# K transposed in place, with its word pairs dealt to four blocks, in a decode kernel of two attention and MLP layers

## The chip, the cores and the metric

The kernel runs on one core of a Trainium2 chip. A core has several engines that work side by side and wait for each other through semaphores: PE multiplies matrices (in the profile PEld is the loading of its stationary operand, "weights", and PE the multiplication itself), DVE works on vectors and transposes small blocks, ACT computes functions and copies, POOL helps with small things, and SP issues the transfers from the chip's main memory. Data is held in SBUF, 128 partitions of addressable rows, and PE writes its results to PSUM, eight banks of 128 x 512 floats.

The metric is the device time of one execution in microseconds. Smaller is better.

## The reference

Two layers are applied twice with the same weights and the same caches: attention A with cached keys and values, then an MLP-like block B. There are 8 sequences of one new token each, model width 448, 16 query heads over 8 cached heads ("groups" below) of 4096 positions and 256 dimensions.

```python
def _A_ref(x, k_cache, v_cache, wq, wo):
    B, Sq, D = x.shape
    Hq, Dh = 16, 256
    q = (x @ wq).reshape(B, Sq, Hq, Dh).transpose(0, 2, 1, 3)
    k = jnp.repeat(k_cache, 2, axis=1)
    v = jnp.repeat(v_cache, 2, axis=1)
    scores = jnp.einsum("bhqd,bhkd->bhqk", q, k) * (Dh ** -0.5)
    p = _softmax(scores, axis=-1)
    o = jnp.einsum("bhqk,bhkd->bhqd", p, v)
    return o.transpose(0, 2, 1, 3).reshape(B, Sq, Hq * Dh) @ wo

x = A_x
x = x + _A_ref(_layernorm(x), k_cache, v_cache, wq, wo)
x = x + _B_ref(_layernorm(x), w1, w2, w3, w4)
x = x + _A_ref(_layernorm(x), k_cache, v_cache, wq, wo)
x = x + _B_ref(_layernorm(x), w1, w2, w3, w4)
```

With one token per sequence, the part of B that shifts along the sequence yields zeros, and its rest is `gelu(layernorm(x) @ w3) @ w4` with two additions. The caches are nearly all of the data: K and V are 128 MiB each, and both layers read them.

## The kernel before

**Units and parts.** A unit is one pass (1 or 2, the first or the second attention), one sequence and one group: 128 units. The cache rows of a unit are cut into four parts of 512 KB, each a tile of 128 partitions x 2048 bf16 elements (eight positions of 256 dimensions per partition). A part is loaded into one of 31 equal buffers, `slots`.

**K kept for the second pass.** A sequence's pass 1 handles its groups; then its MLP and its second query projection are computed, step by step, beside a few units that belong to other sequences (from `ends` to `fence`); then its pass 2 follows. Six of the eight groups (`KEEP`) keep their transposed K in the slots from pass 1 to pass 2, except for two parts that are parked in PSUM (`park`) and copied back by ACT (line 458). The other two groups (`loose`) load K twice. So units come in two kinds: *fresh* ones load four parts of K and four of V, the others V alone. In order of time there are eight fresh opening units, then in turn a short stretch of four (later three) fresh units with the MLP's steps beside them, and a stretch of twelve units, six of them fresh; the last eight units have two fresh ones.

**Transposing K.** PE contracts over partitions, so the dimensions of K have to lie on partitions. `transposes` (lines 470 to 494) takes a loaded part `raw`, reads it as 4-byte words (pairs of neighbouring bf16 elements), and lets DVE transpose 32 x 32 blocks of words, two instructions of 128 x 512 words each (line 486), into a second slot `kt`. A row of K has 128 words. Before the change, block `e` of a row is its words 32e to 32e+31; both the read and the write run over neighbouring words. Parts that are parked are transposed twice, the second time into PSUM (line 491). The slot `raw` is then free and goes back to the list.

**Slots.** `free` is a list of free slots, in the order in which they were freed. `pump` (line 451) issues the next loads of a fixed list, as long as more than `RESERVE` slots are free: one slot is held back, so that a transposition finds its second slot. The planner's table `by` says how many parts must have been transposed at each quarter of a unit; it spreads a stretch's transpositions evenly over the stretch.

**Scores.** `k_part` (line 565) takes a transposed part in 16 matmuls (line 573). The stationary operand is 128 positions wide: its columns stand two elements apart in `kt` (`x` picks the element of the pair, `e` the block). The moving operand is `Qblk`, which holds the two query heads of the group, zero outside their block of 32 partitions. Then come the softmax (lines 585 to 645, with DVE's reductions in lines 588, 606 and 643) and V's part (line 552), a unit later.

**The queries.** `in_mms` multiplies a token's row by `wq` so that the dimensions of a query come out on partitions; `cols` picks the 128 columns of `wq` that make one matmul. For the queries (`pairs`) it takes every second column out of 256. `expand` (line 148) spreads the result into `Qblk`: four matmuls with 0/1 matrices (`rows32`, line 154) repeat 32 partitions four times, and ACT copies the result into place (line 160).

**Order.** The order on each engine is written out by hand in the main loop: in each quarter of a unit, transpositions, the flush of small steps, scores, softmax, V's part, and one step of the MLP. Each engine works through its own list in order; SP issues the loads in the order in which `pump` was called.

Of the kernel before, what the change touches and what calls it, by code (L numbers as in the profile page):

```python
# [8 lines left out]
FP32 = mybir.dt.float32  # L9
# [5 lines left out]

UNIT = 2048
N_SLOTS = 31
RESERVE = 1
KEEP = 6
PARKED = 2  # L20
RUN = 3
# [5 lines left out]
def kernel(  # L27
# [14 lines left out]
    nc = tc.nc  # L42
# [41 lines left out]
    rows32 = consts.tile([128, 4, 4, 32], BF16, name="rows32")  # L84
# [6 lines left out]
    Qblk = [consts.tile([128, RUN, 4, 2, 4, 2], BF16, name=f"Qblk{i}") for i in range(2)]  # L91
# [4 lines left out]
    scb, dnb, pyb = banks[0:2], banks[2], banks[3]  # L96
    park = [[ps1.tile([128, 512], FP32, name=f"park{i}{q}") for q in range(2)] for i in range(PARKED)]
# [19 lines left out]
    def in_mms(pv, big, tail, rows, n, ms, pairs=False):  # L117

        half = n // 2

        def cols(w, k):
            if pairs:
                return w[:, 256 * (k // 2) + k % 2 : 256 * (k // 2) + 256 : 2]
            return w[:, 128 * k : 128 * k + 128]

        for j, m in enumerate(ms):
            for i in range(2):
                for c in range(3):  # L130
                    nc.tensor.matmul(  # L131
                        pv[:, i, j, :],
                        cols(big[:, c, :], m + i * half),
                        rows[:, c, :],
                        start=(i == 0 and j == 0 and c == 0),
                        stop=True,
                        skip_group_check=True,
                    )
            nc.tensor.matmul(  # L139
                pv[:, :, j, :],  # L140
                cols(tail, m),
                rows[:, 3:5, :],
                start=False,
                stop=True,
                skip_group_check=True,
            )

    def expand(blk, qT, n, bank):

        rp = bank[:, 448 : 448 + 16 * n].rearrange("p (g d e h) -> p g d e h", d=4, e=2, h=2)  # L150
        qs = qT.rearrange("p (g h e) -> p g e h", h=2, e=2)
        for db in range(4):
            sel = rows32[:, db].rearrange("p b i -> p (b i)")
            nc.tensor.matmul(rp[:, :, db], sel, qs, start=True, stop=True)  # L154

        for pb in range(4):
            sl = slice(32 * pb, 32 * pb + 32)
            dst = blk[sl, 0:n, :, :, pb, :].rearrange("p g d e h -> p (g d e) h")
            src = rp[sl].rearrange("p g d e h -> p (g d e) h")
            nc.scalar.copy(dst, src)  # L160
# [188 lines left out]
    parked = {(second[-1], 4 - PARKED + i): i for i in range(PARKED)}  # L349
    early = [(1, b, g) for b in range(1, Bn) for g in loose]  # L350
    after = [(2, b, g) for b in range(Bn - 1) for g in loose]
    units = []
# [15 lines left out]
    def fresh(u, s):  # L368

        return u[0] == 1 or u[2] in loose  # L370
# [4 lines left out]
    t = 0  # L375
    while t < n_units:
        p, b, g = units[t]
        n = 1
# [3 lines left out]
        for j in range(parts_):  # L382
            m = n // parts_ + (j < n % parts_)
# [26 lines left out]
    for t in range(n_units):  # L410
        for s in range(4):
            i = 4 * t + s + LAG
            if t in ends:
                i = 4 * t + (6, 6, 7, 7)[s]
            elif t + 1 == n_units:
                i = 4 * t + (5, 5, 6, 7)[s]
# [4 lines left out]
    k = 0  # L421
    for i in range(4 * n_units + 8):
# [4 lines left out]
        t, q = divmod(i + 2, 4)  # L427
# [3 lines left out]
    free = list(slots)  # L431
    raw_of, v_of, kt_of = {}, {}, {}
# [16 lines left out]
    def pump():  # L449
        while loads and len(free) > RESERVE:  # L450
            kind, t, i = loads.pop()
            _, b, g = units[t]
            x = free.pop(0)
            if kind == "p":
                dst = x[:].rearrange("p (e q c x) -> p q c e x", e=4, q=2, c=4)
                for j in range(2):
                    src = park[parked[g, i]][j][:].bitcast(BF16)
                    nc.scalar.copy(dst[:, j], src.rearrange("p (c e x) -> p c e x", c=4, e=4))  # L458
                kt_of[(1, b, g), i] = x
                continue  # L460
            cache, of = (A_k_cache, raw_of) if kind == "k" else (A_v_cache, v_of)
            nc.sync.dma_start(  # L462
                x[:].rearrange("p (c d) -> p c d", d=Dh),
                cache[b, g].rearrange("(p s c) d -> p s c d", s=4, c=8)[:, i],
            )
            of[t, i] = x
            n_loads[0] += 1
            if n_loads[0] >= 8 and extra:
                nc.sync.dma_start(*extra.pop(0))
# [3 lines left out]
    def transposes(i):  # L473


        while len(parts) - len(todo) < by[i]:
            t, s = todo[-1]
            if 4 * t + s > i and ((t, s) not in raw_of or not free):
                return
            todo.pop()  # L480
            raw = raw_of.pop((t, s))
            kt = kt_of[units[t], s] = free.pop(0)
            src = raw[:].bitcast(FP32).rearrange("p (q c e i) -> p q c e i", q=2, c=4, e=4)
            dst = kt[:].bitcast(FP32).rearrange("p (e q c r) -> p q c e r", e=4, q=2, c=4)
            for q in range(2):
                nc.vector.transpose(dst[:, q], src[:, q])  # L486
            _, b, g = units[t]
            if (g, s) in parked:
                for q in range(2):
                    dst = park[parked[g, s]][q][:].rearrange("p (c e r) -> p c e r", c=4, e=4)  # L490
                    nc.vector.transpose(dst, src[:, q])
            free.append(raw)
            pump()


    pts, scs, mzs, pos = {}, {}, {}, {}
# [9 lines left out]
    def make_blocks(t):  # L506

        if t in runs and t not in ready:
            p, b, g = units[t]
            if p == 1 or b in q_done:  # L510
                x, n = runs[t]
                qT = qT1[:, :, b] if p == 1 else qT2[:, :, b % 3]
                expand(Qblk[x], qT[:, 4 * g : 4 * (g + n)], n, scb[t % 2])
                ready.add(t)

    def head_out(t):
# [25 lines left out]
    def v_part(t, s):  # L542
        if s == 0:
            at = PO + 4 * (t % n_po)
            pos[t] = pyb[:, at : at + 4].rearrange("p (k h) -> p k h", h=2)
            if t == n_po // 2:
                nc.vector.memset(pyb[:, PO : PO + 4 * (n_units - n_po)], 0.0)
        v = v_of.pop((t, s))
        vv = v[:].rearrange("p (c d) -> p c d", d=Dh)
        for c in range(8):  # L550
            for k in range(2):
                nc.tensor.matmul(  # L552
                    pos[t][:, k, :],
                    vv[:, c, 128 * k : 128 * k + 128],
                    pts[t][:, 8 * s + c, :],
                    start=(t == 0 and s == 0 and c == 0 and k == 0),
                    stop=True,
                    skip_group_check=True,
                )
        free.append(v)  # L560
        pump()

    def k_part(t, s):
        u = units[t]
        p, b, g = u
        if s == 0:
            scs[t] = scb[t % 2][:, 0:64].rearrange("p (c b h) -> p c b h", b=4, h=2)
        key = (u if fresh(u, s) else (1, b, g)), s
        ktv = kt_of[key][:].rearrange("p (e c m x) -> p e c m x", e=4, c=2, x=2)
        for c in range(2):  # L570
            for db in range(4):
                for x in range(2):
                    nc.tensor.matmul(  # L573
                        scs[t][:, 2 * s + c, :, :],
                        ktv[:, db, c, :, x],
                        Qblk[run_of[t][0]][:, run_of[t][1], db, x, :, :],
                        start=(db == 0 and x == 0),
                        stop=(db == 3 and x == 1),
                    )
        if p == 2 or g in loose or (g, s) in parked:  # L580
            free.append(kt_of.pop(key))
            pump()
# [117 lines left out]

    pump()
    make_blocks(0)

    last = n_units - 1
    for t in range(n_units + 1):
        cur = t < n_units
        for q in range(4):
            i = 4 * t + q
            if cur:
                if t in fence and q == 0:  # L710
                    while dense:
                        dense_next()
                    flush()
                    make_blocks(t)
                late = q == 0 and t and not beside[t]
                if beside[t]:
                    transposes(i)
                flush()
                if not late and not beside[t]:
                    transposes(i)  # L720
                k_part(t, q)
# [3 lines left out]
            if cur and late:  # L725
                transposes(i)
# [14 lines left out]
            if q > 1:  # L741
                make_blocks(t + 1)
# [36 lines left out]
    for i in (1, 0):  # L779
        f, e = TWICE[i]  # L780
# [24 lines left out]
    for c in range(4):  # L805
        yp = (scb[0] if c % 2 else dnb)[:, 32 * c : 32 * c + Bn]
        for m in range(HC):
# [4 lines left out]
                start=(m == 0),  # L812
                stop=(m == HC - 1),
# [4 lines left out]
    for c in range(4):  # L818
        sel = ident if c < 3 else rows32[:, 2:4, 0, :]
# [37 lines left out]
```

## Time and profile before

| | |
|---|---|
| median of 3 runs | 1136.29 us (1134.88 to 1136.89) |
| the profiled execution | 1134.93 us, its span 1133.2 us |
| busy PE / PEld / DVE / ACT / POOL | 689.6 / 624.5 / 556.7 / 293.1 / 104.2 us |
| read from main memory | 446.77 MB, 394 GB/s over the span |
| transpositions of K into slots (line 486) | 640, 415.9 us of DVE, 688 ns each |
| transpositions into the park (line 491) | 32, 20.4 us |
| score matmuls (line 573) | 8192, with 8192 weight loads of 104 ns each, overlapping |

The profile is of one execution. Its groups are instructions of one line with one shape: number, busy time, mean duration, and the idle time of the engine just ahead of them with what ended it. The durations of one engine's instructions can overlap: 16 weight loads of 104 ns each are issued in 0.43 us. A stage's row gives the busy time of each engine in a stretch of the span.

### The profile page before, as it was taken

The page shows a single profiled execution, that of the slowest core. Times are in us where ns is not written, and L with a number is a line of the kernel's source. Part 1 is how long each engine was busy: PE and PEld are TensorE (multiplying, and loading weights), DVE is VectorE, ACT ScalarE, POOL GpSimd, SP SyncE. Part 2 cuts the span into 40 slices and gives each one's busy share as a digit, 9 for nine tenths or more (in the row PEclk, how much of TensorE's full clock was granted, in tenths as well). Part 3 has the DMA queues.
Part 4 walks back from the last instruction along what each step waited for, and adds up shares of the span by engine and source line. Part 5 has one row for each costly group of instructions (what it writes and reads, how often), then busy time and mean ns, then how long its engine had stood idle before and what let it go on. Part 6 is the DMA issues. An engine that isn't in the chain of part 4 may idle for free.

```text
span 1133.2 us, 46689 instructions
## 1 busy us (share of the span) xinstructions
PE 689.6 (61%) x20665; PEld 624.5 (55%) x20665; DVE 556.7 (49%) x1305; ACT 293.1 (26%) x1280; POOL 104.2 (9%) x156
## 2 busy tenths in 40 slices
PE   3155665657656576565656666565765666565665
PEld 3144655556555565565655565565655565565665
DVE  5265645446454554545545464545544454546332
ACT  1012123222322223221232214222232214221241
POOL 0000010001000010000000010000100000000011
DMA  9999999999999999999999999999999999999993
GB/s 362 383 418 417 407 399 416 417 405 387 417 417 416 398 392 415 416 417 374 402 417 416 417 375 387 417 417 415 358 416 416 416 384 409 417 416 406 355 417 132
DMA packets 127194, 449.80 MB, mean 397 GB/s; under 512 B 13568, under 2 KB 19600, under 8 KB 126608
## 3 DMA queue, kind: packets, MB, share of 16 engines
q1 hardware_dynamic: 126992, 446.83, 98.9%
q8 instruction: 161, 2.64, 0.8%
q14 instruction: 41, 0.34, 0.1%
HBM read 446.77 MB, written 0.01 MB: 394 GB/s over the span
## 4 chain that ended last, share of the span: by engine, by line
DMA 71%; PE 13%; DVE 5%; issue 5%; ACT 3%; SPq 2%; POOL 0%; POOLq 0%; DVEq 0%; ACTq 0%
DMA slot<-in_A_v_cache_dram 42%; DMA slot<-in_A_k_cache_dram 28%; PE bank L552 3%; DVE slot L486 3%; PE bank L573 3%; PE bank L131 2%; SPq L462 2%; ACT pt L636 2%; PE bank L231 1%; PE bank L632 1%; ACT pe L609 1%; DVE small L606 1%; PE bank L596 0%; PE bank L622 0%; PE bank L139 0%
## 5 line engine op out<-in xcount | busy, mean ns | idle before, releaser
L552 PE MATMUL bank<-pt,slot 128*128 128x2 bf16 x8192 | 302.0, 166 | 361.3 <-DMA slot<-in_A_v_cache_dram 327.3
L552 PEld LDWEIGHTS <-slot 128*128 128x128 bf16 x8192 | 265.6, 105 | 414.7 <-DMA slot<-in_A_v_cache_dram 380.4
L486 DVE STREAM_TRANSPOSE slot<-slot 128x512 f32<-128x512 f32 x640 | 415.9, 688 | 146.7 <-DMA slot<-in_A_k_cache_dram 131.6
L573 PE MATMUL bank<-Qblk,slot 128*128 128x8 bf16 x8192 | 294.9, 168 | 24.2 <-issue 15.4
L573 PEld LDWEIGHTS <-slot 128*128 128x128 bf16 x8192 | 263.7, 104 | 28.7 <-issue 22.5
L644 POOL TENSOR_TENSOR small<-small 128x2 f32<-128x2 f32 x128 | 89.3, 698 | 970.7 <-DVE small L643 970.7
L609 ACT ACTIVATE pe<-bank,small 128x32 bf16<-128x32 f32 x256 | 61.1, 296 | 449.9 <-DVE small L606 449.9
L636 ACT CAST pt<-bank 32x64 bf16<-32x64 f32 x512 | 103.8, 203 | 142.8 <-PE bank L632 138.4
L606 DVE TENSOR_REDUCE small<-bank 128x2 f32<-128x256 f32 x128 | 54.0, 422 | 154.0 <-PE bank L596 154.0
L643 DVE TENSOR_REDUCE small<-bank 128x2 f32<-128x64 f32 x128 | 28.4, 221 | 160.9 <-ACT pt L636 119.6
L588 DVE TENSOR_REDUCE small<-bank 128x2 bf16<-128x64 f32 x128 | 27.2, 213 | 88.1 <-PE bank L573 88.0
L160 ACT CAST Qblk<-bank 32x48 bf16<-32x48 f32 (+2 forms) x200 | 37.4, 187 | 101.1 <-PE bank L154 87.3
L632 PE MATMUL bank<-pe,rows 128*128 128x64 bf16 x512 | 51.0, 241 | 0.0
L596 PE MATMUL bank<-rows,small 128*128 128x128 bf16 x256 | 48.0, 291 | 1.9 <-DVE small L588 1.9
L522 ACT ACTIVATE OT<-bank,small 128x2 bf16<-128x2 f32 x128 | 26.9, 261 | 70.1 <-PE bank L552 68.9
L175 PEld LDWEIGHTS <-wo_sb 128*128 128x128 bf16 x1152 | 35.4, 104 | 6.8 <-issue 6.8
L632 PEld LDWEIGHTS <-rows 128*128 128x128 bf16 x512 | 33.7, 124 | 8.6 <-issue 7.5
L175 PE MATMUL bank<-OT,wo_sb 128*128 128x1 bf16 x1024 | 33.1, 165 | 5.0 <-ACT OT L522 5.0
L131 PEld LDWEIGHTS <-wq_sb 128*128 128x128 bf16 x864 | 29.9, 106 | 8.5 <-DMA wq_sb<-in_A_wq_dram 4.5
L622 PE MATMUL bank<-pe,small 128*128 128x64 bf16 x128 | 27.3, 213 | 7.2 <-ACT pe L609 4.4
L458 ACT COPY slot<-park 128x1024 bf16<-128x1024 bf16 x32 | 30.8, 1015 | 3.1 <-PE bank L552 2.9
L522 ACT ACTIVATE qT<-bank,small 128x2 bf16<-128x2 f32 x128 | 27.0, 265 | 7.8 <-PE bank L552 4.2
(108 smaller groups left out, 321.3 us busy)
## 6 DMA issues: line engine op xcount, KB each, us to landing
slot<-in_A_v_cache_dram SPq DMA_DIRECT2D x512, 512.0 KB, 9.9
slot<-in_A_k_cache_dram SPq DMA_DIRECT2D x320, 512.0 KB, 9.9
wo_sb<-in_A_wo_dram SPq DMA_DIRECT2D x4, 896.0 KB, 9.3
wq_sb<-in_A_wq_dram SPq DMA_DIRECT2D x3, 1024.0 KB, 6.9
w_sb<-in_B_w_dram SPq DMA_DIRECT2D x1, 1568.0 KB
w_sb<-in_B_w_dram SPq DMA_DIRECT2D x3, 448.0 KB, 10.3
wq_tl<-in_A_wq_dram SPq DMA_DIRECT2D x2, 256.0 KB, 10.1
w_tl<-in_B_w_dram SPq DMA_DIRECT2D x2, 112.0 KB, 9.3
```

The source lines that it names most:

```text
L131: nc.tensor.matmul(pv[:, i, j, :], cols(big[:, c, :], m + i * half), rows[:, c, :], start=(i == 0 and j == 0 and c == 0), stop=True, skip_ ...
L175: nc.tensor.matmul(y[:, c, :], chunk(wo_sb[:, k, :], c), o[:, k, :], start=False, stop=True, skip_group_check=True,)
L486: nc.vector.transpose(dst[:, q], src[:, q])
L522: nc.scalar.mul(o, pos[t][:, :, h], rzs[t % 2][:, h : h + 1])
L552: nc.tensor.matmul(pos[t][:, k, :], vv[:, c, 128 * k : 128 * k + 128], pts[t][:, 8 * s + c, :], start=(t == 0 and s == 0 and c == 0 and k ...
L573: nc.tensor.matmul(scs[t][:, 2 * s + c, :, :], ktv[:, db, c, :, x], Qblk[run_of[t][0]][:, run_of[t][1], db, x, :, :], start=(db == 0 and x ...
L596: nc.tensor.matmul(mzs[t][:, 128 * h : 128 * h + 128], pm[:, h : h + 1].to_broadcast([128, 128]), ident, start=True, stop=True,)
L606: nc.vector.tensor_reduce(nm, mx, AX.X, ALU.max, negate=True)
L609: nc.scalar.activation(pe[:].rearrange("p c b h -> p h (c b)")[:, h], scs[t].rearrange("p c b h -> p h (c b)")[:, h], ACT.Exp, bias=nm[:, ...
L632: nc.tensor.matmul(pp[:, c], sel, pe[:], start=True, stop=True)
L636: nc.scalar.copy(pts[t][sl].rearrange("p (k c) h -> p k c h", c=4), pp[sl, :, :, pb, :].rearrange("p c k h -> p k c h"),)
L644: nc.gpsimd.tensor_tensor(out=rzs[t % 2], in0=zs, in1=mone, op=ALU.pow)
```

## The change

The blocks of a row are chosen differently. Words are dealt to the four blocks in turn: block `e` of a row now consists of words e, e+4, e+8 and so on. Read and write of the transposition use the same pattern, so the block is written over itself in the slot in which it was loaded; no second slot is taken, the slot is not freed after the transposition but only after its scores, and `RESERVE` is 0. A part that is parked is first transposed into the park and then in place. In the scores the stationary operand's columns stand eight elements apart instead of two. To match, `cols` takes every eighth column out of 1024 of `wq`, so that a matmul's result holds four heads with 32 partitions each, and `expand` takes, for each of the four heads, the rows that hold it: a matmul for each block of 32 partitions, over the groups of one parity. The numbers of loads, their order, and the places of all transpositions in DVE's list stay the same.

```diff
-RESERVE = 1
+RESERVE = 0
...
         def cols(w, k):
             if pairs:
-                return w[:, 256 * (k // 2) + k % 2 : 256 * (k // 2) + 256 : 2]
+                return w[:, 1024 * (k // 8) + k % 8 : 1024 * (k // 8) + 1024 : 8]
             return w[:, 128 * k : 128 * k + 128]
...
-    def expand(blk, qT, n, bank):
+    def expand(blk, qT, g0, n, bank):
 
         rp = bank[:, 448 : 448 + 16 * n].rearrange("p (g d e h) -> p g d e h", d=4, e=2, h=2)
-        qs = qT.rearrange("p (g h e) -> p g e h", h=2, e=2)
-        for db in range(4):
-            sel = rows32[:, db].rearrange("p b i -> p (b i)")
-            nc.tensor.matmul(rp[:, :, db], sel, qs, start=True, stop=True)
+        rq = bank[:, 448 : 448 + 16 * n].rearrange("p (g x h) -> p g x h", x=8, h=2)
+        for k in range(4):
+            gs = [g for g in range(g0, g0 + n) if g % 2 == k // 2]
+            if gs:
+                sel = rows32[:, k].rearrange("p b i -> p (b i)")
+                qs = qT[:, 8 * (gs[0] // 2) : 8 * (gs[-1] // 2) + 8]
+                nc.tensor.matmul(
+                    rq[:, gs[0] - g0 : gs[-1] - g0 + 1 : 2, :, k % 2],
+                    sel,
+                    qs.rearrange("p (g x) -> p g x", x=8),
+                    start=True,
+                    stop=True,
+                )
...
             if kind == "p":
-                dst = x[:].rearrange("p (e q c x) -> p q c e x", e=4, q=2, c=4)
                 for j in range(2):
                     src = park[parked[g, i]][j][:].bitcast(BF16)
-                    nc.scalar.copy(dst[:, j], src.rearrange("p (c e x) -> p c e x", c=4, e=4))
+                    nc.scalar.copy(x[:, 1024 * j : 1024 * j + 1024], src)
...
             t, s = todo[-1]
-            if 4 * t + s > i and ((t, s) not in raw_of or not free):
+            if 4 * t + s > i and (t, s) not in raw_of:
                 return
             todo.pop()
             raw = raw_of.pop((t, s))
-            kt = kt_of[units[t], s] = free.pop(0)
-            src = raw[:].bitcast(FP32).rearrange("p (q c e i) -> p q c e i", q=2, c=4, e=4)
-            dst = kt[:].bitcast(FP32).rearrange("p (e q c r) -> p q c e r", e=4, q=2, c=4)
-            for q in range(2):
-                nc.vector.transpose(dst[:, q], src[:, q])
+            kt_of[units[t], s] = raw
+            src = raw[:].bitcast(FP32).rearrange("p (q c i e) -> p q c e i", q=2, c=4, e=4)
             _, b, g = units[t]
             if (g, s) in parked:
                 for q in range(2):
-                    dst = park[parked[g, s]][q][:].rearrange("p (c e r) -> p c e r", c=4, e=4)
+                    dst = park[parked[g, s]][q][:].rearrange("p (c i e) -> p c e i", c=4, e=4)
                     nc.vector.transpose(dst, src[:, q])
-            free.append(raw)
-            pump()
+            for q in range(2):
+                nc.vector.transpose(src[:, q], src[:, q])
...
-                expand(Qblk[x], qT[:, 4 * g : 4 * (g + n)], n, scb[t % 2])
+                expand(Qblk[x], qT, g, n, scb[t % 2])
...
-        ktv = kt_of[key][:].rearrange("p (e c m x) -> p e c m x", e=4, c=2, x=2)
+        ktv = kt_of[key][:].rearrange("p (c m e x) -> p e c m x", e=4, c=2, x=2)
```

## The prediction

> **What bounds the kernel now.** I read the page's sections on queues and on the chain first, then the costly groups, then the table by stage.
>
> ```profile
> span 1133.2 us, 46689 instructions
> ...
> PE 689.6 (61%) x20665; PEld 624.5 (55%) x20665; DVE 556.7 (49%) x1305; ACT 293.1 (26%) x1280; POOL 104.2 (9%) x156
> ...
> q1 hardware_dynamic: 126992, 446.83, 98.9%
> ...
> DMA 71%; PE 13%; DVE 5%; issue 5%; ACT 3%; SPq 2%; POOL 0%; POOLq 0%; DVEq 0%; ACTq 0%
> ...
> L486 DVE STREAM_TRANSPOSE slot<-slot 128x512 f32<-128x512 f32 x640 | 415.9, 688 | 146.7 <-DMA slot<-in_A_k_cache_dram 131.6
> L573 PE MATMUL bank<-Qblk,slot 128*128 128x8 bf16 x8192 | 294.9, 168 | 24.2 <-issue 15.4
> L573 PEld LDWEIGHTS <-slot 128*128 128x128 bf16 x8192 | 263.7, 104 | 28.7 <-issue 22.5
> ```
>
> The loads bound the kernel: the transfer engines are busy for 98.9% of the span, and the chain that ended last is 71% DMA. DVE works half of the time, and three quarters of that is L486, the transposition of K. At 417 GB/s, the best rate of a slice, 446.83 MB need 1072 us, so 61 us of the span are not at the full rate. Where they are, the table by stage shows. I cut the span at the ends of units (the 128 reductions of L588), at the points where the planner cuts its rows. The first row is the eight opening units; then follow, in the order of time, a stretch of four units that load K, a stretch of twelve of which six load K, a stretch of three, and the last eight units. All instructions come first, L486 alone last:
>
> ```profile
> 0.00:107.30 107.30, 41.78 (x1177) 35.86 (x1177) 53.05 (x125) 17.88 (x76) 6.55 (x16) 1.00 1.01 394
> 107.30:148.80 41.50, 27.82 (x827) 25.66 (x827) 24.67 (x67) 8.63 (x42) 4.04 (x6) 1.00 1.02 405
> 284.10:377.30 93.20, 56.72 (x1717) 50.53 (x1715) 43.85 (x91) 27.53 (x118) 8.37 (x12) 1.00 1.03 417
> 647.90:683.30 35.40, 22.93 (x689) 21.36 (x690) 18.88 (x56) 6.31 (x30) 3.34 (x5) 1.00 0.99 383
> 1059.90:1113.30 53.40, 36.71 (x1177) 35.34 (x1175) 16.68 (x40) 19.58 (x80) 5.59 (x8) 1.00 1.00 395
> ...
> 107.30:148.80 41.50, 19.61 (x31) 1.00 1.02 405
> 284.10:377.30 93.20, 32.41 (x50) 1.00 1.03 417
> ```
>
> Columns: stretch, length, busy PE, PEld, DVE, ACT, POOL, granted clock, DMA share, GB/s. In the twelve-unit stretches the loads run at 417 and nothing else matters. In the short ones (four of four units, mean 42.2 us; four of three, mean 34.4 us) they drop to 380 to 405: there the MLP's steps alternate between PE and DVE, and slots come free late. DVE is nearest to its limit there, with 24.67 of 41.50 us.
>
> **What the new access costs.** K's blocks are now read and written with one 4-byte word in every 16 bytes, and so are the weights of L573 and of the q projection (one 2-byte element in every 16 bytes). Before, both were contiguous, or had a step of two elements. No transposition or weight load of the trace has a step of 16 bytes. The nearest rows are these:
>
> ```profile
> L686 DVE COPY X<-bank 128x32 f32<-128x32 f32 x1 | 0.3, 266 | 0.0
> L692 DVE CAST slot<-bank 128x24 bf16<-128x24 f32 x1 | 0.2, 181 | 1.3 <-PE bank L690 1.3
> L824 DVE CAST slot<-bank 8x256 bf16<-8x256 f32 x1 | 0.4, 412 | 0.3 <-PE bank L820 0.3
> L772 DVE CAST slot<-slot 128x32 bf16<-128x32 f32 x1 | 0.2, 228 | 0.0
> L797 DVE TENSOR_TENSOR slot<-slot,slot 128x32 f32<-128x32 f32 x1 | 0.2, 192 | 0.7 <-POOL slot L784 0.7
> ...
> L154 PE MATMUL bank<-qT,rows x4: 182/183/183, 17.1 to 17.2; 128*128 128x12 bf16 x4
> L154 PE MATMUL bank<-qT,rows x4: 175/175/176, 85.2 to 85.3; 128*128 128x8 bf16 x4
> L154 PE MATMUL bank<-qT,rows x4: 172/172/173, 171.2 to 171.3; 128*128 128x12 bf16 x4
> ```
>
> These are rows by line and form, and one line's instructions in three windows (the third reads qT2, 6 bytes apart). L692 and L824 write contiguously: 231 ns for 232 more elements, 1.0 ns each, so 32 elements would take 189 ns. L686 writes 32 floats 16 bytes apart in 266 ns: 77 ns more, 3.4 ns an element. L772 writes elements 16 bytes apart in 228 ns against 192 ns for the same number in L797: 2.1 ns an element. PE reads qT1 with a step of 16 bytes in L154: four more columns cost 8 ns, 2.0 ns each. So 2.0 to 3.4 ns an element in place of 1.0. I take 2.4, nearer to the two that agree. Both streams of a transposition are strided now; I count them as running side by side, and what they cost if they add up is a rival.
>
> [...]
>
> **Part by part.**
>
> *Transposition, L486 and the parked copies.* 640 and 32 instructions, as many as before and in the same places, except that a parked block is now copied ahead of its own transposition. One costs 19.61/31 = 0.633 us of DVE now, and 0.633 + 512 x 1.4 ns = 1.35 us then (bounds: 0.633 if steps are free, 0.633 + 512 x 2.4 ns = 1.86 us). DVE's other work in a stage is its row less L486. To it come the waits for PE that DVE keeps in each unit's softmax: the groups of L606, L643 and L588 idle 154.0, 160.9 and 88.1 us over 128 units, 3.1 us a unit. Much of this is only slack; I keep 1.2 us a unit, L606's part.
> - Four-unit stretch: 5.1 + 31 x 1.35 + 4.8 = 51.8 us, against 42.2: +9.6, four times: 38.
> - Three-unit stretch: 4.5 + 23 x 1.35 + 3.6 = 39.2 us, against 34.4: +4.8, four times: 19.
> - Twelve-unit stretch (50 transpositions and 4 copies to the park): 9.0 + 54 x 1.35 + 14.4 = 96.3 us, against 92.3: +4, seven times: 28.
> - First stage: work on K begins at 14.7 us; 14.7 + 7.8 + 70 x 1.35 + 2 = 119 us, against 107.3: +11.7.
> - Last stage: 16.7 + 16 x 0.72 = 28 of 53 us: nothing.
> Together 97 us. What is late then: reductions queue behind transpositions of 2.7 us a part, PE waits for transposed K, and slots come free late, so SP's loads wait. DVE takes DMA's place as the bound of the short stretches.
>
> *Weight loads of L573 and of the q projection.* 8192 and 1008. They issue 0.43 us per 16 now, 27 ns each, with a step of two elements, just as V's contiguous ones in L552. [...] I take 53 ns, doubled, near to what PE's own strided read shows in L154. A twelve-unit stretch then has 56.7 + 768 x 0.027 = 77 us of PE work, a four-unit one 27.8 + 352 x 0.027 = 37 us, below DVE's 96 and 52: hidden, as long as DVE is the slower one. Not hidden: 112 loads ahead of the first scores, 3 us, and in the last stage 50.4 us of PE work in 53.4 us, where I put 3 us. Together 6.
>
> *One slot.* A block needs no second slot, and none is held back: all 31 slots hold loads, one more than now, 1.26 us of loading (512 KB at 417 GB/s). SP's queue has the same loads in the same order. What goes is its wait for L486 to release a slot (67.5 us in 71 waits); the slot is released by PE's scores instead, and SP waits for those. Where DVE bounds, loading ahead is worth nothing: 0 us. Bounds: 0, and the 29 us that the rate's dips cost between the first 60 and the last 35 us (windows of 20 us, each one's shortfall from 417 GB/s).
>
> *The rest.* Building the query blocks takes eight matmuls fewer (0.2 us), some with 16 columns in place of 12, and writes PSUM with a step of two words; 44 waits of ACT stand behind it, so at most 1 us either way. ACT's copies out of the park (32 x 1.015 us) keep their number of elements: 0, inside ACT's 74% idle time. The transposition's wait for a free slot goes (10.7 us of idle DVE on PE), which pays only where DVE bounds, and is within the kept 1.2 us.
>
> The sum: 97 + 6 = 103 us on the profiled execution's 1134.9 us (span 1133.2 and 1.7 around it; 1.4 below the median of the runs): 1238, stated as 1240.
>
> **Rivals.**
>
> *Steps cost little, the slot decides (faster).* If an element takes at most about 1.9 ns, a transposition is under 1.1 us, a four-unit stretch 5.1 + 34 + 4.8 = 44 us at most, and with steps free nothing is lost; each of the eight dips then gets a block of 1.26 us more to live on, perhaps twice. 1134.9 - 8 x 1.26 = 1125 us; 1105 if all 29 us come back. This turns to slower once an element costs 2 ns. Against it stand L686, L772 and L154. [...]
>
> *Mild.* 2.0 to 2.2 ns: a transposition of 1.15 to 1.25 us, hidden in the twelve-unit stretches, and 6 us or less in each short one: 1139 us, with the slot's gain, to 1180.
>
> *Heavy.* From 2.8 ns up: L686's 3.4 ns, or reads and writes that add up: 1.86 us. The four stages' sums grow by 25, 16, 31 and 47 us: 100 + 66 + 220 + 47 = 433, 1568 us; at 3 ns (1.66 us) about 1435.
>
> [...]
>
> **How the numbers follow.** The forecast (2.2 to 2.7 ns) has 0.45, on its own 1180 to 1340 us, by the same four sums; mild 0.12; heavy 0.15; weight loads 0.08; the faster case 0.20, of which 0.03 falls within 0.2% of no change (about 2.3 us, what a measurement here can tell). Faster 0.17, same 0.03, slower 0.80. The range leaves out the lowest of the faster case (0.08) and most of the two heavy ones (0.12): 1122 to 1430.
>
> **What would show it.** L486's mean: 688 ns now, about 1.4 us if right, under 1.1 if the faster rival holds, near 1.9 if the heavy one does. [...] DVE's busy share: 49% now, near 85%. The rate in the short stretches falls to about 310 GB/s, and there the chain goes through DVE L486 instead of DMA. I am wrong if transpositions with a step keep their time, or if DVE's part of the softmax costs much more than 1.2 us a unit once it is full.

## The result, and the profile after

The changed kernel takes 1166.81 us (1165.79 to 1168.16, 4 runs), the kernel before 1135.59 us beside it: 1.0277 times as long, 95% interval 1.0257 to 1.0297, so 31 us slower. Slower was forecast, but by 104 us.

From the page of the changed kernel: busy times, the load queue, the chain that ended last, and the groups that answer to those shown of before (lines have moved: L486 is now L498, L573 is L578).

```profile
span 1164.0 us, 46597 instructions
...
PE 968.8 (83%) x20657; PEld 929.3 (80%) x20657; DVE 813.9 (70%) x1305; ACT 294.4 (25%) x1280; POOL 104.3 (9%) x156
...
q1 hardware_dynamic: 126992, 446.83, 96.8%
...
DMA 58%; PE 21%; DVE 15%; issue 2%; SPq 2%; ACT 1%; POOL 0%; POOLq 0%; DVEq 0%; ACTq 0%
...
L498 DVE STREAM_TRANSPOSE slot<-slot 128x512 f32<-128x512 f32 x640 | 678.5, 1119 | 50.4 <-DMA slot<-in_A_k_cache_dram 49.6
L578 PE MATMUL bank<-Qblk,slot 128*128 128x8 bf16 x8192 | 574.9, 202 | 25.6 <-DVE slot L498 18.6
L578 PEld LDWEIGHTS <-slot 128*128 128x128 bf16 x8192 | 543.5, 167 | 30.3 <-DVE slot L498 23.7
L131 PEld LDWEIGHTS <-wq_sb 128*128 128x128 bf16 x864 | 62.7, 169 | 4.3 <-DMA wq_sb<-in_A_wq_dram 4.3
```

A transposition takes 1119 ns where it took 688. A score weight load takes 167 ns where it took 104, and 16 of them are issued in 0.97 us instead of 0.43. PE and DVE together got 536 us more to do; the kernel lost 31. The chain says where: DMA's share falls from 71% to 58%, DVE's rises from 5% to 15% and PE's from 13% to 21%.

The same stretches as in the prediction, cut at the ends of units of the changed kernel (columns as there): the eight opening units, a four-unit, a twelve-unit and a three-unit stretch, and the last eight units.

```profile
0.00:109.90 109.90, 64.86 (x1217) 60.03 (x1217) 79.17 (x125) 17.86 (x76) 6.57 (x16) 1.00 1.01 397
245.20:291.70 46.50, 38.64 (x805) 37.12 (x803) 36.18 (x67) 8.89 (x42) 4.04 (x6) 1.00 0.98 382
291.70:383.10 91.40, 79.97 (x1745) 76.62 (x1742) 64.98 (x91) 27.25 (x116) 8.37 (x12) 1.00 1.02 410
657.30:697.10 39.80, 32.28 (x665) 30.82 (x663) 27.18 (x56) 6.33 (x30) 3.34 (x5) 1.00 0.93 362
1088.00:1144.40 56.40, 52.92 (x1179) 52.09 (x1177) 22.88 (x41) 19.52 (x80) 5.58 (x8) 1.00 0.94 366
```

| profiled execution | first | eight short | seven long | last | rest |
|---|---|---|---|---|---|
| before | 107.3 | 306.4 | 646.2 | 53.4 | 19.9 |
| changed | 109.9 | 343.8 | 634.3 | 56.4 | 19.6 |

The short stretches, where the MLP runs beside fresh units, lose 37.4 us. The long ones *gain* 11.9. Neither PE (39 of 46.5 us) nor DVE (36) fills a short stretch, which is the first thing to explain.

### The profile page after: what moved, and what is told of

It is laid out like the page before. It is cut to its first block, busy times and chain, and to the rows that moved or that the text cites. A ratio compares the mean times of both kernels' runs of the same rounds, so it can differ in the third digit from the quotient of the medians.

```text
span 1164.0 us, 46597 instructions
## 1 busy us (share of the span) xinstructions
PE 968.8 (83%) x20657; PEld 929.3 (80%) x20657; DVE 813.9 (70%) x1305; ACT 294.4 (25%) x1280; POOL 104.3 (9%) x156
## 4 chain that ended last, share of the span: by engine, by line
DMA 58%; PE 21%; DVE 15%; issue 2%; SPq 2%; ACT 1%; POOL 0%; POOLq 0%; DVEq 0%; ACTq 0%
DMA slot<-in_A_v_cache_dram 38%; DMA slot<-in_A_k_cache_dram 18%; DVE slot L498 11%; PE bank L578 10%; PE bank L557 4%; PE bank L131 4%; SPq L470 1%; DMA w_sb<-in_B_w_dram 1%; DVE small L611 1%; DVE park L496 1%; PE bank L139 1%; PE bank L601 1%; DMA wq_sb<-in_A_wq_dram 1%; PE bank L184 1%; PE bank L240 0%
## 5 line engine op out<-in xcount | busy, mean ns | idle before, releaser
L498 DVE STREAM_TRANSPOSE slot<-slot 128x512 f32<-128x512 f32 x640 | 678.5, 1119 | 50.4 <-DMA slot<-in_A_k_cache_dram 49.6
L578 PE MATMUL bank<-Qblk,slot 128*128 128x8 bf16 x8192 | 574.9, 202 | 25.6 <-DVE slot L498 18.6
L578 PEld LDWEIGHTS <-slot 128*128 128x128 bf16 x8192 | 543.5, 167 | 30.3 <-DVE slot L498 23.7
L557 PEld LDWEIGHTS <-slot 128*128 128x128 bf16 x8192 | 279.3, 106 | 134.3 <-DMA slot<-in_A_v_cache_dram 128.4
L131 PEld LDWEIGHTS <-wq_sb 128*128 128x128 bf16 x864 | 62.7, 169 | 4.3 <-DMA wq_sb<-in_A_wq_dram 4.3
L131 PE MATMUL bank<-small,wq_sb 128*128 128x1 bf16 x768 | 55.4, 198 | 0.0
L496 DVE STREAM_TRANSPOSE park<-slot 128x512 f32<-128x512 f32 x32 | 33.9, 1108 | 0.0
```

The costliest lines, as they stand in the source:

```text
L131: nc.tensor.matmul(pv[:, i, j, :], cols(big[:, c, :], m + i * half), rows[:, c, :], start=(i == 0 and j == 0 and c == 0), stop=True, skip_ ...
L498: nc.vector.transpose(src[:, q], src[:, q])
L557: nc.tensor.matmul(pos[t][:, k, :], vv[:, c, 128 * k : 128 * k + 128], pts[t][:, 8 * s + c, :], start=(t == 0 and s == 0 and c == 0 and k ...
L578: nc.tensor.matmul(scs[t][:, 2 * s + c, :, :], ktv[:, db, c, :, x], Qblk[run_of[t][0]][:, run_of[t][1], db, x, :, :], start=(db == 0 and x ...
```

## The experiments

Three accesses have become strided: the transpositions (T below), the score weights (K) and the wq columns (W). The first two theories blame one engine each: in the expectations, theory T means the transpositions on DVE, and theory W all weight loads on PE, those of K and of wq. Four kernels undo the three accesses one at a time, and all at once. The kernel before, run beside each of the kernels below, took 1133.4 to 1133.8 us, beside the result 1135.6; so a difference of 1 or 2 us between kernels measured apart is not to be read.

**Score weights two elements apart again**

```diff
-        ktv = kt_of[key][:].rearrange("p (c m e x) -> p e c m x", e=4, c=2, x=2)
+        ktv = kt_of[key][:].rearrange("p (e c m x) -> p e c m x", e=4, c=2, x=2)
```

> The changed kernel, with the weights of the score matmuls read two elements apart again. The blocks stay dealt by fours, so the scores add products of dimensions that do not belong together; the amount of work is the same. Theory W (the weight loads cost the time: 66 ns in place of 32 each, in PE's list): L578's weight loads fall back to about 104 ns in mean and 0.43 us per 16, the short stretches fall from 46.5 and 39.8 us to about 42 and 35, the first and last stage lose their 3 us each, and the time is 1128 to 1142 us. Theory T (the transpositions cost the time: DVE's 1.12 us each, ahead of the MLP's steps in DVE's list): short stretches stay at 45 to 46.5 and 38 to 40 us, time 1155 to 1167 us.

Measured: 1153.6 us, 1.0173 times before (1.0150 to 1.0197). K's weight loads are back at 105 ns; 13 us came back.

**Transpositions over neighbouring words, still in place**

```diff
-            src = raw[:].bitcast(FP32).rearrange("p (q c i e) -> p q c e i", q=2, c=4, e=4)
+            src = raw[:].bitcast(FP32).rearrange("p (q c e i) -> p q c e i", q=2, c=4, e=4)
...
-                    dst = park[parked[g, s]][q][:].rearrange("p (c i e) -> p c e i", c=4, e=4)
+                    dst = park[parked[g, s]][q][:].rearrange("p (c e r) -> p c e r", c=4, e=4)
```

> The changed kernel, with the transpositions over neighbouring words (blocks of 32 words side by side, still in place). The weights are still read eight elements apart, so the scores add products of dimensions that do not belong together; the amount of work is the same. Theory T: L498 falls to about 690 ns, the short stretches to about 42 and 35 us, time 1128 to 1142 us. Theory W: L498 falls all the same, but the time stays at 1155 to 1167 us. If both prices matter in about equal parts, this run and the one with cheap score weights each lie near 1150.

Measured: 1147.76 us, 1.0116 (1.0087 to 1.0144); 19 us came back. The chain on its page shows that DVE is out of it and PE, at 29%, is not:

```profile
DMA 65%; PE 29%; SPq 2%; ACT 2%; issue 1%; DVE 1%; POOL 0%; POOLq 0%; ACTq 0%; DVEq 0%
...
L498 DVE STREAM_TRANSPOSE slot<-slot 128x512 f32<-128x512 f32 x640 | 413.4, 685 | 102.2 <-DMA slot<-in_A_k_cache_dram 102.1
```

**wq columns two apart**

```diff
-                return w[:, 1024 * (k // 8) + k % 8 : 1024 * (k // 8) + 1024 : 8]
+                return w[:, 256 * (k // 2) + k % 2 : 256 * (k // 2) + 256 : 2]
```

> The changed kernel, with the columns of wq taken two apart, as before. The queries' dimensions then stand in another order than K's; the amount of work is the same. The 112 weight loads of each second query projection fall from about 60 ns to 27 ns each, 3.7 us in each short stretch and once at the start. Theory W, with the projection on the stretch's chain: 8 x 3 to 4 us and 3 us at the start, 1132 to 1143 us. Theory T: at most 10 us, 1157 to 1167 us.

Measured: 1147.21 us, 1.0114 (1.0087 to 1.0140); 20 us came back, as much as from the transpositions, and from 1008 weight loads against K's 8192.

**All three undone: the slot alone**

The three edits above together.

> The changed kernel without any of its strided reads: transpositions in place over neighbouring words, score weights and wq columns two elements apart. The scores add products of dimensions that do not belong together; the amount of work is the same. What is left of the change is the slot. If the slot is worth what the faster rival said (a block of 1.26 us in each of eight dips), 1120 to 1128 us; if a slot is worth nothing, 1133 to 1138 us.

Measured: 1131.45 us, 0.9974 (0.9961 to 0.9987), 2 to 3 us faster than before. That lies between the two cases of the expectation: the slot helps, by less than a third of what the faster rival gave it.

So neither theory stood: each access alone gave back 13 to 20 us, 52 in sum, where undoing all gave back 35. Either prices hide behind each other, or something absorbs the first of them. The next three kernels keep one strided access each.

**Only the transpositions strided**

```diff
-                return w[:, 1024 * (k // 8) + k % 8 : 1024 * (k // 8) + 1024 : 8]
+                return w[:, 256 * (k // 2) + k % 2 : 256 * (k // 2) + 256 : 2]
...
-        ktv = kt_of[key][:].rearrange("p (c m e x) -> p e c m x", e=4, c=2, x=2)
+        ktv = kt_of[key][:].rearrange("p (e c m x) -> p e c m x", e=4, c=2, x=2)
```

> One slot and in place, with only the transpositions strided: score weights and wq columns are read two elements apart, so the scores add products of dimensions that do not belong together; the amount of work is the same. Removed from the whole change one at a time, the three strided accesses gave back 13 (score weights), 19 (transpositions) and 20 us (wq), 52 together, where removing all gave back 35. Theory C (one chain: the MLP's steps of a short stretch pass through DVE and PE in turn, so that every price on it adds up): each access alone costs its share of 35, here 12 to 19 us over the slot alone, 1143 to 1150 us. Theory S (slack: each alone is covered by the loads, and only two together exceed them): 0 to 6 us, 1131 to 1138 us.

Measured: 1136.52 us, 1.0024 (1.0006 to 1.0042): 5 us over the slot alone.

**Only the score weights strided** (the changed kernel with the edits of T and W undone, as above)

> One slot and in place, with only the score weights strided (eight elements apart); transpositions run over neighbouring words and wq columns are taken two apart, so the scores add products of dimensions that do not belong together; the amount of work is the same. Theory C: 8 to 13 us over the slot alone, 1139 to 1145 us. Theory S: 0 to 4 us, 1131 to 1136 us.

Measured: 1132.83 us, 0.9994 (0.9976 to 1.0012): 1 us over the slot alone.

**Only the wq columns strided** (the edits of T and K undone)

> One slot and in place, with only the wq columns strided (eight apart); transpositions over neighbouring words and score weights two elements apart, so the queries' dimensions stand in another order than K's; the amount of work is the same. Theory C: 13 to 20 us over the slot alone, 1144 to 1152 us. Theory S: 0 to 6 us, 1131 to 1138 us.

Measured: 1134.83 us, 1.0015 (1.0000 to 1.0029): 3 us over the slot alone.

Theory S (slack, in the expectations above) holds in the total: alone, 5, 1 and 3 us by the medians, 2 to 6 by the ratios; together 35. The stretches of the profiled executions, one for each kernel, in us, show that theory C (one chain) holds as well, in the short ones:

| strided | eight short | over the slot alone | seven long | time |
|---|---|---|---|---|
| none (the slot alone) | 301.9 | | 643.0 | 1131.45 |
| K | 312.1 | 10.2 | 632.5 | 1132.83 |
| T | 314.4 | 12.5 | 634.6 | 1136.52 |
| W | 315.7 | 13.8 | 634.3 | 1134.83 |
| T, K | 324.2 | 22.3 | 634.8 | 1147.21 |
| T, W | 333.8 | 31.9 | 635.7 | 1153.60 |
| K, W | 334.6 | 32.7 | 628.5 | 1147.76 |
| T, K, W | 343.8 | 41.9 | 634.3 | 1166.81 |

In the short stretches the prices add up, or come to more: T and K 22.7, measured 22.3; T and W 26.3, measured 31.9; K and W 24.0, measured 32.7; all three 36.5, measured 41.9. The long stretches give some 7 to 15 us back, once, and the second and third access get nothing more from them. The first 10 us or so that the short stretches lose are thus nearly free: while they are late the loads go on as long as there are slots, and the long stretches start further ahead. The rates show it. By rate times length, the eight short stretches move 229 blocks of 512 KB with the slot alone and 236 to 241 with one strided access; the seven long ones, which use 504 blocks, move 505 with the slot alone, 495 to 499 with one strided access and 491 in the changed kernel. Why they give back no more is not shown. It is not that they stand at the full rate of the loads: 504 blocks of 1.257 us are 633.5 us, near the 634 of most rows, but K and W together need only 628.5, and the long stretches of the changed kernel run at 399 to 412 GB/s, not 417. In one of them, 429.6 to 520.0, the dip comes at its start: from 429.6 to 440.0 the rate is 372 GB/s and PE is busy for 10.39 of 10.40 us, and after that the rate is 415 to 418.

**Why the prices add up although neither engine is full.** The chain through the short stretch from 520.0 to 566.5 us of the changed kernel (start, length, what), its DVE part and then some of its PE part:

```profile
535.74 2.07 DVE slot L498 x2
537.81 0.10 DVE small L226
...
538.53 2.13 DVE slot L498 x2
...
540.86 1.34 DVE slot L498 x2
...
546.21 2.07 DVE slot L498 x2
...
553.43 0.59 PE bank L240 x2
554.01 0.36 PE bank L131 x6
554.38 0.06 PE bank L139
...
556.54 0.96 PE bank L578 x16
557.50 0.23 PE bank L601 x2
557.73 0.40 PE bank L557 x16
558.13 0.37 PE bank L131 x6
```

And the engines' busy times in the two parts of it:

```profile
535.00:553.40 18.40, 15.20 (x338) 14.54 (x335) 17.92 (x45) 3.95 (x19) 2.09 (x3) 1.00 0.97 373
553.40:566.50 13.10, 13.07 (x243) 13.07 (x244) 7.15 (x10) 2.82 (x13) 1.26 (x2) 1.00 0.96 355
```

Up to 535 us the stretch waits for loads (the chain stands on a block of V until 531.7). The rest has two parts with a full engine each. As long as the MLP's steps stand in DVE's list among the transpositions, DVE is busy for 17.92 of 18.40 us. Then comes the second query projection, and PE is busy for 13.07 of 13.10 us, with wq's weight loads and K's in turn. Over the whole stretch PE is busy for 38.55 and DVE for 36.06 of 46.5 us, as if each had about a fifth of its time to spare.

That this is so in all eight short stretches, and which access lengthens which part, the other profiled executions show. Each short stretch is cut here at the first matmul of the second query projection (L131), and the eight are summed, in us:

| strided | up to the projection | from there on |
|---|---|---|
| none (the slot alone) | 240.3 | 61.5 |
| K | 245.9 | 66.3 |
| T | 259.1 | 55.1 |
| W | 240.1 | 75.8 |
| T, K | 261.5 | 62.8 |
| T, W | 257.6 | 76.1 |
| K, W | 247.1 | 87.6 |
| T, K, W | 256.3 | 87.6 |

T lengthens only the first part, and W only the second. K costs 6 us in the first, and in the second 5 us without W but 12 beside it. With K and W strided, PE is busy for the whole of the second part in all eight stretches, and T changes nothing in it. In the 18 us ahead of the cut DVE is busy for 98% in the four-unit and 90% in the three-unit stretches of the changed kernel, and for 66 to 77% with K and W alone. Only a part of each price counts, though. T makes the 31 or 23 transpositions of a stretch 13 or 10 us longer (0.43 us each), of which the first parts show 1.2 to 2.4 us a stretch in the mean. That fits the wait for loads up to 535 us: as long as it lasts, a longer transposition is covered.

**The small steps ahead of the transpositions**

```diff
-                if beside[t]:
-                    transposes(i)
                 flush()
-                if not late and not beside[t]:
+                if not late:
                     transposes(i)
```

> The whole change, with the MLP's small steps put ahead of the transpositions in DVE's list in the short stretches too (as they are elsewhere). If the steps are late in the short stretches because they stand behind two transpositions of 1.1 us each, this shortens the short stretches by 1 to 3 us each, 1145 to 1160 us. If DVE then waits for PE ahead of the transpositions instead, and the scores wait for the blocks, the short stretches stay or grow, 1166 to 1185 us.

Measured: 1167.37 us, 1.0306 (1.0268 to 1.0343), the same as the changed kernel. Where the steps stand in DVE's list does not matter for the time. An engine that is full whatever the order would explain that; this run does not prove it.

**The changed kernel with one slot less**

```diff
-N_SLOTS = 31
+N_SLOTS = 30
```

> The whole change with 30 slots, so that the loads have as many slots as before the change. If the slot is worth the same here as without the strided accesses (2 to 3 us there), 1168 to 1171 us; if it is worth a block's load in each of the eight short stretches, which are late now, 1175 to 1180 us; if nothing, 1166 to 1168 us.

Measured: 1176.85 us, 1.0380 (1.0356 to 1.0404): 10 us more than with 31. The profiled stretches: short 346.1 us, long 642.9, against 343.8 and 634.3. So the slot is worth 10 us here: the time of the expectation's second case, but most of it in the long stretches and not in the short ones. With as many slots for loads as before, the strided accesses cost 43 us; the slot the change gains pays for 10 of them.

**The kernel before with one slot less** (the same edit)

> The kernel before with 30 slots, one less. A slot was worth 2 us without strided accesses (in place against two slots) and 10 us in the whole change. If a slot's worth rises with how late the short stretches are, it is worth 2 to 4 us here, 1135 to 1139 us; if the number of slots itself matters and 30 are just too few, 1142 to 1147 us.

Measured: 1142.19 us, 1.0073 (1.0046 to 1.0100), 8 us more. Without strided accesses each slot is worth less than the one before: 8 us for the 31st of the old kernel, 2 to 3 for the one that in-place work adds to it. So the number of slots counts, as the second case of the expectation has it. It is not all that counts: the step from 30 to 31 slots for loads is worth 2 to 3 us without the strided accesses and 10 with them, which points to the lateness of the short stretches as well.

**What the strided accesses cost by themselves.** Two kernels show it line by line. The first is the kernel before, with one side of each transposition strided:

```diff
-            dst = kt[:].bitcast(FP32).rearrange("p (e q c r) -> p q c e r", e=4, q=2, c=4)
-            for q in range(2):
-                nc.vector.transpose(dst[:, q], src[:, q])
+            far = raw[:].bitcast(FP32).rearrange("p (q c i e) -> p q c e i", q=2, c=4, e=4)
+            fat = kt[:].bitcast(FP32).rearrange("p (q c i e) -> p q c e i", q=2, c=4, e=4)
+            near = kt[:].bitcast(FP32).rearrange("p (q c e r) -> p q c e r", q=2, c=4, e=4)
+            nc.vector.transpose(near[:, 0], far[:, 0])
+            nc.vector.transpose(fat[:, 1], src[:, 1])
```

> The kernel before with two slots, where the first transposition of a part reads one word in four and writes neighbouring words, and the second reads neighbouring words and writes one word in four. The blocks of the two halves are laid out differently, so the scores add products of dimensions that do not belong together; the amount of work is the same. In the whole change, where both are strided, one took 1119 ns against 688. If reads and writes run side by side and cost the same, both lines show about 1.1 us; if only one side costs, one line stays at 690 ns and the other shows about 1.1 us; if they add, each shows about 0.9 us.

Its groups (L487 reads strided and writes neighbours, L488 the other way round):

```profile
L487 DVE STREAM_TRANSPOSE slot<-slot 128x512 f32<-128x512 f32 x320 | 347.9, 1087 | 83.3 <-DMA slot<-in_A_k_cache_dram 74.6 <-PE bank L554 2.6 <-issue 2.3
L488 DVE STREAM_TRANSPOSE slot<-slot 128x512 f32<-128x512 f32 x320 | 340.8, 1065 | 0.0
```

Either side alone costs nearly as much as both (1119 ns): the two prices do not add up, as if reads and writes ran side by side. The kernel takes 1147.85 us, one run, 14 us more than the kernel before. In place, with one slot more for loads, strided transpositions alone came to 1136.52 us; that too speaks for a slot that is worth more where the short stretches are late.

The second is the slot alone, with four steps for the score weights:

```diff
...
+                    kk = kt_of[key][:]
+                    to = scs[t][:, 2 * s + c, :, :]
+                    qb = Qblk[run_of[t][0]][:, run_of[t][1], db, x, :, :]
+                    if db == 0:
+                        nc.tensor.matmul(to, kk[:, 256 * c + x : 256 * c + 256 : 2], qb, start=(x == 0), stop=False)
+                    elif db == 1:
+                        nc.tensor.matmul(to, kk[:, 512 * c + x : 512 * c + 512 : 4], qb, start=False, stop=False)
+                    elif db == 2:
+                        nc.tensor.matmul(to, kk[:, 1024 * c + x : 1024 * c + 1024 : 8], qb, start=False, stop=False)
+                    else:
+                        nc.tensor.matmul(to, kk[:, 8 * c + x : 2048 : 16], qb, start=False, stop=(x == 1))
```

> One slot, transpositions over neighbouring words, and the score weights read with four steps on four lines: 2, 4, 8 and 16 elements (4, 8, 16 and 32 bytes). The scores add products that do not belong together; the amount of work is the same. Step 2 shows 104 ns and step 8 about 167 ns in mean. If what counts is that two neighbouring columns share a 16-byte line, step 4 stays at 104 ns and step 16 is as dear as step 8; if the price grows with the step, step 4 lies between 104 and 167 ns and step 16 above 167.

From its timeline (start, length of the group, line); L582, L584, L586 and L588 have steps of 2, 4, 8 and 16 elements, two loads each:

```profile
302.50 0.13 PEld L582 LDWEIGHTS <-slot 128*128 128x128 bf16 x2
302.55 0.15 PEld L584 LDWEIGHTS <-slot 128*128 128x128 bf16 x2
302.61 0.21 PEld L586 LDWEIGHTS <-slot 128*128 128x128 bf16 x2
302.72 0.22 PEld L588 LDWEIGHTS <-slot 128*128 128x128 bf16 x2
302.84 0.15 PEld L582 LDWEIGHTS <-slot 128*128 128x128 bf16 x2
302.92 0.15 PEld L584 LDWEIGHTS <-slot 128*128 128x128 bf16 x2
```

From start to start, two loads take 0.05, 0.06, 0.11 and 0.12 us. In mean over the run's 2048 loads of each line, one lasts 111, 116, 155 and 162 ns. A part of a dear load's time seems to fall to the load behind it: the two loads of step 2 take 0.05 us to the next start when they follow V's (302.50 to 302.55), and 0.08 when they follow those of step 16 (302.84 to 302.92). So a step of 4 elements (8 bytes) is free or nearly so, 0.06 against 0.05 us; 8 and 16 elements (16 and 32 bytes) cost about the same, 0.11 and 0.12 us, twice as much and a little more. The times fall as in the expectation's first case; that lines of 16 bytes are the reason, the run does not show. The kernel takes 1133.41 us, one run.

## Why the prediction was wrong

- **The sign, and that 16-byte steps cost time on DVE and PE:** right. The faster rival's turning point, 2 ns an element, was wrong: at 1.84 ns the kernel is 31 us slower. The measured time lies in the stated range, but outside the forecast's own 1180 to 1340 us. It is among the mild rival's times, but not by its reasons: at 1.84 ns the price is the faster rival's (at most about 1.9), and the time is not.
- **"So 2.0 to 3.4 ns an element in place of 1.0. I take 2.4":** too high, and the bounds too. (1119 - 688)/512 = 0.84 ns more make 1.84 ns. Copies of 32 elements were a poor measure; the nearest row, 2.0, was PE's, another engine's, which is luck. That the prices of the two streams do not add up was right (1087 and 1065 ns for one side, 1119 for both).
- **The sum by stages, 97 us:** this is the step that failed. It set the work of one engine, DVE, against the whole length of a stretch. With the right price, 0.633 + 0.43 = 1.06 us, the same sums give 42.8 us for a four-unit stretch (then 42.2), 32.5 for a three-unit one (34.4), 81 for a long one (92.3) and 98.7 for the first (107.3): nearly nothing. The profiled stretches are 45.0 to 46.5, 39.8, 90.6 in mean and 109.9. So the price was too high, and behind it a term was missing: DVE fills only the first part of a short stretch and PE the second, and what lengthens either part lengthens the stretch, whichever engine has the larger sum. By the runs, T costs 5 us alone and 19 beside K and W (1166.81 against 1147.76), where 97 were forecast; K and W together cost 30 us beside T (1166.81 against 1136.52), where 6 were.
- **"Hidden, as long as DVE is the slower one" (weight loads, 6 us):** wrong. K and W together cost 32.7 us in the short stretches, without T 16 us in the time. The price, taken as 53 ns, is 61 (0.97 us per 16). The 0.08 for weight loads as the bound rests on no price that a run shows: steps of 16 and 32 bytes cost at most these 61 ns a load, and with them PE is busy for 80 of 91 us in a long stretch. The 112 loads of wq in a stretch were put beside DVE; they are on the chain after DVE's part has ended. They got 112 x 34 ns = 3.8 us longer, and the second part of a stretch shows 1.8 to 3.1 us of it. In the last stage 3 us were forecast and 3.0 came, in part by chance: with the slot alone, nothing strided, it is already 55.3 us against 53.4.
- **Long stretches, +4 us each:** they got 1.7 us shorter each. At 1.12 us a transposition DVE fills 65 of 91 us there, and the chain through one of them (429.6 to 520.0) is 90% loads.
- **"Where DVE bounds, loading ahead is worth nothing: 0 us":** wrong, since it does not bound the long stretches. The slot is worth 10 us in the changed kernel, as much as the faster rival gave it but for another reason, and 2 to 3 us without the strided accesses, which is that rival's case.
- **What was to show it:** L498's mean lies between the mild and the faster case, DVE is busy for 70% (85 forecast), the short stretches run at 360 to 382 GB/s (310 forecast). That the chain would go through DVE's transpositions there was right for the first part of a stretch.

## What to carry to other kernels

When steps of two engines alternate, cut the stretch finer until one engine is full in each piece; 83% of PE and 78% of DVE over a whole stretch can be two pieces at 100 and 97%, and then both prices count. This kernel, bound by its loads, took a small delay for next to nothing, while free slots let the loads run ahead, so single costs of 1 to 5 us made 35 together. Before an in-place layout is chosen for the sake of a buffer, ask for what a buffer is worth (here 2 to 3 us) and for the step that it forces on every reader (here 16 bytes: 1119 ns against 688 for DVE's transposition, 1.6 times, and 0.97 us against 0.43 for 16 of PE's weight loads, 2.3 times).

## What the runs showed of the hardware

- A weight load of 128 columns takes 27 ns from start to start at a step of 4 bytes (0.43 us per 16, kernel before), about 30 at 8 bytes (0.06 us for two, the four steps on four lines), and 55 to 61 ns at 16 and 32 bytes (0.97 us per 16 in the changed kernel; 0.11 and 0.12 us for two in the other).
- A transposition of 128 x 512 words takes 688 ns over neighbouring words and 1065 to 1119 ns with one word in four on either side or both. The second side adds 3 to 5%.
- One more slot of 512 KB for loads was worth 8 us (kernel before, 30 to 31 slots), 2 to 3 (in place, nothing strided) and 10 (the changed kernel, 30 to 31), with the same loads.
